# Second buffers for early keys and queries, wider idle matmuls, later stores: one change to an attention and two-MLP kernel

## The chip, the cores and the metric

The kernel runs on one core of one Trainium2 chip. The metric is the device time of one execution in microseconds (us). The kernel before has a median of 1110.62 us over three runs, from 1107.44 to 1112.64.

## What is computed

The reference is chunked local attention with eight memory slots, then two feed-forward layers with different gates, all in float32:

```python
for c in range(nc):                      # 24 chunks of 32 queries
    q_c = q[:, :, c_start:c_end]
    k_full = concatenate([mem_k, k[:, :, l_start:r_end]], axis=2)   # 8 + up to 56 keys
    v_full = concatenate([mem_v, v[:, :, l_start:r_end]], axis=2)
    a = softmax(q_c @ k_full.T / 8)
    out[:, :, c_start:c_end] = a @ v_full
x = out.transpose(0, 2, 1, 3).reshape(3072, 512)
h = x @ w_in1;  x = (s * relu(h) ** 2 + b) @ w_out1           # w_in 512 x 2048, w_out 2048 x 512
h = x @ w_in2;  return (h * sigmoid(1.702 * h)) @ w_out2
```

## The kernel before

**Tiles and blocks.** The 3072 tokens are 24 tiles of 128. Four tiles make a block of 512. The hidden size 2048 is 16 slices `j` of 128 columns. Each slice has a weight tile of w_in and one of w_out.

**Precision.** Every float32 matmul of the feed-forward layers is three matmuls on split operands: a value is cast to a high part, and the rest is subtracted out of it (names that end in h and l, such as `xh`, `xl`, `wih`, `wil`, `gh`, `gl`). So each weight tile has to be prepared: it is loaded as 64-bit words into a ring of three `st` buffers (L326), ScalarE takes an absolute value (L332) and a scaled low word (L342), VectorE clamps (L338), shifts (L346), adds (L350) and puts the sign in (L354), then ScalarE casts the high part (L223) and VectorE subtracts the rest (L312). Working copies `u` have a ring of four.

**Attention.** `attend(u)` does one tile (tiles 0 to 3) or two: load keys, queries, values (L403, all on SyncE's queue except the first two query loads, which ScalarE issues), scores `sc` (L418), row maximum `top` (L435), subtraction into the query buffer `qe` (L438), exponential (L443), transposes `pp` (L451), copy to `px` (L223), sums `den` (L461 to L465), products with the values `o` (L479), normalisation (L484), transposes `xx` (L493), and the split into `xh` and `xl` (L223, L510). `k`, `v`, `qe` and `px` have one buffer each, which holds a pair of tiles `g` = 0, 1, 2, ...: the loads of a pair wait until the pair before is done with the buffer. PSUM is shared too: `sc`, `pp`, `o` and `xx` of tiles 0 and 2 and of all the pairs from (4, 5) on use one region; tiles 1 and 3 use that of the accumulator `accA`.

**First layer.** `step(i)` is a unit: hidden product `ph` of one slice and one block (12 matmuls, L602 to L604), gates `r` (L609, L616, L613 or L620), split `gh`, `gl` (L624, L628), and two units later the output product into `accA` and `accB` (12 matmuls, L640). `VISITS` orders the units: block 0 with slices 0 to 4 (slices 0 and 1 as half blocks, so that tiles 0 and 1 are enough to begin), block 1 with 0 to 4, block 1 with 5 to 15, block 0 with 5 to 15, then blocks 2 and 3. Unit 16 is block 1, slice 9. Blocks 4 and 5 and the whole second layer go through `seven(s)`, a Strassen-like scheme of seven products on prepared w_in slices, which `combine(p)` and `pair(p)` store to DRAM (`wch`, `wcl`) and `stream` reads again.

**Order.** The instruction order of each engine is fixed when the program is built. A planner (class `Plan`) gives each step a due time and a modelled duration and orders all steps; the steps are then emitted in that order on one queue per engine, and each waits only for the data and buffers that it really touches. Where the planner expects TensorE to be idle before the first output product (`plan.first`), it puts in idle matmuls on zeros (L1183), one of 128 columns for each 0.24 us (`BEAT`). `after=` is for the planner: it moves a step in the order and adds no wait of its own.

**What the change touches in `combine`.** For each pair of slices it stores the prepared tiles `wih`, `wil` (L725, four stores: 256, 256, 128 and 128 KB) as soon as they exist, and much later sums them (L736 to L755, two `u` and two `st` buffers) and stores the sums (L764).

**Gates in `seven`.** Two of the four gate sets of each pair of slices (`mine` false) take a `u` buffer for `r` (L999, L1002, L1008), cast and subtract it into a `gq` buffer, and store that to DRAM, except the last sets of a round, which stay in SBUF.

## Time and profile before

| what | value |
|---|---|
| median of three runs | 1110.62 us |
| profiled execution, time | 1112.08 us |
| profiled execution, span in the trace | 1110.2 us |
| TensorE matmul busy | 1088.7 us (98%) |
| VectorE busy | 711.0 us (64%) |
| ScalarE busy | 494.2 us (45%) |
| granted TensorE clock, mean | 1.000 |
| chain that ended last: TensorE's share | 92% |

TensorE is busy in nearly all of the span, so what is left to look at is where it is not, or where it is busy with matmuls on zeros. Both lie almost wholly in the first 82 us, which the rows below show by stretch. A busy TensorE in the profile counts overlapping matmuls, so the view that lists waits is read beside it.

### The profile page before, as it was taken

Reading aid. Unit: us, or ns where it says so; the run is one execution under the profiler, and the core shown is the slowest. Engines: PE = TensorE matmul, PEld = TensorE weight load, DVE = VectorE, ACT = ScalarE, POOL = GpSimd, SP = SyncE. Lnnn points to the kernel's source line nnn. Section 1 sums busy time; section 2 is a strip of 40 time slices with the busy share of each in tenths; the row PEclk is TensorE's granted clock in tenths of the full one; section 3 lists DMA queues with packets and bytes.
Section 4 is the critical chain, followed back from the end, with each engine's and each line's share of the span. In section 5 each row is a group of like instructions: output and inputs, shape, how many; then the busy total and the mean of one; then the engine's idle time right before and its main releaser. Section 6 shows DMA issues by size and latency. Waiting matters only on the chain.

```text
span 1110.2 us, 20092 instructions
## 1 busy us (share of the span) xinstructions
PE 1088.7 (98%) x7852; PEld 897.8 (81%) x7852; DVE 711.0 (64%) x1241; ACT 494.2 (45%) x842; POOL 0.7 (0%) x6
## 2 busy tenths in 40 slices
PE   8879999999999999999999999999999999999998
PEld 7768887888878788888888888888888888888886
DVE  6888988878778688687881455660555760655610
ACT  4678865555445455566640433330433430333310
POOL 0000000000000000000000000000000000000000
PEclk9999999999999999999999999999999999999999
DMA  8776627756678783888999965574755574654154
GB/s 326 245 258 209 208 105 248 259 193 219 208 275 267 265 301 117 312 294 279 318 323 382 322 203 200 183 260 144 246 188 201 202 246 155 203 190 142 76 191 150
DMA packets 119406, 252.99 MB, mean 228 GB/s; under 512 B 12816, under 2 KB 29200, under 8 KB 119312
## 3 DMA queue, kind: packets, MB, share of 16 engines
q1 hardware_dynamic: 119024, 251.19, 66.1%
q8 instruction: 62, 1.02, 0.4%
q10 hardware_dynamic: 288, 0.52, 0.1%
q14 instruction: 32, 0.26, 0.1%
HBM read 169.87 MB, written 81.79 MB: 227 GB/s over the span
## 4 chain that ended last, share of the span: by engine, by line
PE 92%; DMA 3%; DVE 2%; issue 1%; ACT 1%; SPq 0%; ACTq 0%; DVEq 0%
PE accA L1059 16%; PE accB L1059 16%; PE accA L640 7%; PE accB L640 7%; PE ph L981 5%; PE ph L983 5%; PE ph L982 5%; PE ph L602 5%; PE ph L603 5%; PE ph L604 5%; PE pb L983 4%; PE pb L981 4%; PE pb L982 4%; DMA st<-w_in 2%; PE o L479 1%; PE sc L418 1%
## 5 line engine op out<-in xcount | busy, mean ns | idle before, releaser
L997 ACT ACTIVATE r<-ys 128x512 f32<-128x512 f32 x72 | 45.5, 632 | 107.6 <-DVE ys L1094 81.2
L1083 DVE TENSOR_TENSOR ys<-pb,ys 128x512 f32<-128x512 f32 x32 | 22.0, 686 | 91.6 <-DMA out<-y 58.7
L602 PE MATMUL ph<-xh,wih 128*128 128x512 f32 (+1 forms) x200 | 79.3, 396 | 0.6 <-DVE xh L223 0.6
L603 PE MATMUL ph<-xl,wih 128*128 128x512 f32 (+1 forms) x200 | 76.6, 383 | 0.7 <-DVE xl L510 0.7
L604 PE MATMUL ph<-xh,wil 128*128 128x512 f32 (+1 forms) x200 | 76.4, 382 | 0.0
L223 ACT COPY y<-accA 128x512 f32<-128x512 f32 x20 | 10.9, 590 | 138.5 <-issue 84.4
L609 ACT ACTIVATE r<-ph 128x512 f32<-128x512 f32 (+1 forms) x66 | 38.5, 584 | 60.4 <-PE ph L604 54.2
L624 ACT CAST gh<-r 128x512 fp32r<-128x512 f32 (+1 forms) x66 | 40.2, 609 | 47.8 <-PE accB L640 31.2
L1094 DVE TENSOR_TENSOR ys<-pb,ys 128x512 f32<-128x512 f32 x32 | 22.1, 691 | 53.9 <-PE pb L983 53.3
L1006 DVE TENSOR_TENSOR r<-ph,r 128x512 f32<-128x512 f32 x24 | 16.6, 691 | 62.2 <-ACT r L997 62.2
L1059 PE MATMUL accA<-woh,gh 128*128 128x512 f32 x138 | 54.0, 391 | 0.0
L1059 PE MATMUL accA<-woh,gl 128*128 128x512 f32 x138 | 53.9, 390 | 0.0
L1059 PE MATMUL accB<-woh,gh 128*128 128x512 f32 x138 | 53.7, 389 | 0.0
L1059 PE MATMUL accA<-wol,gh 128*128 128x512 f32 x138 | 53.7, 389 | 0.0
L1059 PE MATMUL accB<-woh,gl 128*128 128x512 f32 x138 | 53.7, 389 | 0.0
L1059 PE MATMUL accB<-wol,gh 128*128 128x512 f32 x138 | 53.7, 389 | 0.0
L640 PE MATMUL accA<-gl,woh 128*128 128x512 f32 (+1 forms) x132 | 50.9, 385 | 2.2 <-DVE gl L628 2.2
L1019 ACT CAST gh<-r 128x512 fp32r<-128x512 f32 x64 | 39.8, 622 | 29.1 <-DVE r L1006 21.7
L342 ACT ACTIVATE st<-st 128x512 f32<-128x512 uint32 x64 | 42.8, 676 | 22.4 <-DMA st<-w_out 10.7
L640 PE MATMUL accA<-gh,woh 128*128 128x512 f32 (+1 forms) x132 | 51.4, 389 | 1.3 <-ACT gh L624 1.3
L640 PE MATMUL accB<-gl,woh 128*128 128x512 f32 (+1 forms) x132 | 50.6, 383 | 1.2 <-issue 1.2
L640 PE MATMUL accB<-gh,woh 128*128 128x512 f32 (+1 forms) x132 | 51.0, 387 | 0.0
(210 smaller groups left out, 2973.6 us busy)
## 6 DMA issues: line engine op xcount, KB each, us to landing
gd<-gq SPq DMA_DIRECT2D x56, 512.0 KB, 2.7
wih<-wch SPq DMA_DIRECT2D x96, 256.0 KB, 3.5
wil<-wcl SPq DMA_DIRECT2D x96, 256.0 KB, 3.8
st<-w_in SPq DMA_DIRECT2D x32, 512.0 KB, 5.4
st<-w_out SPq DMA_DIRECT2D x32, 512.0 KB, 5.0
back<-gd SPq DMA_DIRECT2D x56, 256.0 KB, 3.1
k<-k_w SPq DMA_DIRECT2D x24, 512.0 KB, 5.6
v<-v_w SPq DMA_DIRECT2D x24, 512.0 KB, 6.1
```

Of the source, the lines that this page charges most:

```text
L342: nc.scalar.activation(out=lo.bitcast(F32), in_=lo, func=AF.Copy, scale=2.0**-51, bias=2.0)
L602: nc.tensor.matmul(ph, wh, xh, start=(k == 0), stop=False)
L603: nc.tensor.matmul(ph, wh, xl, start=False, stop=False)
L604: nc.tensor.matmul(ph, wl, xh, start=False, stop=(k == KT - 1))
L624: nc.scalar.copy(out=T["g", i][0], in_=T["r", i])
L640: nc.tensor.matmul(o, lt, rh, start=fresh and x == 0, stop=(done and x == 2))
L981: nc.tensor.matmul(ph, wh, xh, start=first and i == 0, stop=False, skip_group_check=True)
L982: nc.tensor.matmul(ph, wh, xl, start=False, stop=False, skip_group_check=True)
L983: nc.tensor.matmul(ph, wl, xh, start=False, stop=i == 1, skip_group_check=True)
L997: nc.scalar.activation(out=T[rk], in_=src(), func=AF.Sigmoid, scale=GATE)
L1019: nc.scalar.copy(out=T[key][0], in_=T[rk])
L1059: nc.tensor.matmul(a, lt, rh, start=n == 0 and x == 0, stop=n == NF - 1 and x == 2)
```

## The change

Six edits; none changes what is computed.

1. Pairs `g` = 1 (tiles 2 and 3) and `g` = 3 (tiles 6 and 7), counted from one the tiles 3, 4, 7 and 8, get a second `k` and `qe` buffer in a pool of their own (`att2`). `v` and `px` stay single.
2. The space of that pool is handed on to the weight tiles `wz` (w_in of slices 12 to 15) when attention of those pairs is done; the preparation of these four tiles now comes after that.
3. Idle matmuls have 512 columns, with one narrower matmul for the rest.
4. `plan.first` is the first four output products, and idle matmuls end before whichever comes first.
5. The four stores of prepared slices of pair `p` (L725) come after the output product of unit 16 + `p`. The sum of the second tile goes into the `st` buffer, where it took a `u` buffer.
6. The last two gate sets of the round `s` = 0 work in place in `ys` and take no `u` buffer.

```diff
-                idle = min(starts[i], starts[self.first]) - clock
+                idle = min(starts[i], *(starts[x] for x in self.first)) - clock
...
+    pool_b = tc.tile_pool(name="att2", bufs=1)
+    sets = [att, pool_b.__enter__()]
+    home = {1: 1, 3: 1}
...
-        d = op(need, {"act": 0.62}, ..., after=[d], alloc=[(tag, w)], uses=[("u", i)])
+        d = op(need, {"act": 0.62}, ..., after=[d] + (o_open if tag == "wz" else []), alloc=[(tag, w)], uses=[("u", i)])
...
-            T[name, g] = att.tile([P, 2, HP, P] if name in ("qe", "px") else [P, 2, HP, CT, D], F32, tag=name, name=name)
+            T[name, g] = (sets[home.get(g, 0)] if name in ("k", "qe") else att).tile([P, 2, HP, P] if name in ("qe", "px") else [P, 2, HP, CT, D], F32, tag=name, name=name)
...
-            return {"alloc": [(name, (name, g))]}
+            return {"alloc": [(name + "1" if name in ("k", "qe") and g in home else name, (name, g))]}
...
+        end_ = [o_unit[16 + p]]
-        done = [op(need, {"sp": 0.75}, keep(v, w0, slice(0, 512), slice(0, 2)), after=first[v:v + 1], uses=[w0]) for v in range(2)]
+        done = [op(need, {"sp": 0.75}, keep(v, w0, slice(0, 512), slice(0, 2)), after=first[v:v + 1] + end_, uses=[w0]) for v in range(2)]
...
+                    T["s", p] = stp.tile([P, 4, 256], F32R, tag="st", name="st")
+                    x = T["s", p].bitcast(F32)[:, 2:4].rearrange("p n d -> p (n d)")
...
+            there = not (mine or away or m)
+                T[rk] = src() if there else (gp if mine else stp).tile(
+                    [P, 512], F32, tag="r" if mine else "u", name="r", bufs=1 if mine else 4)
...
+    o_open.append(op(-1, {"none": 0.0}, follow("att2", "wz", bufs=1), after=two_ops))
...
-            for _ in range(e):
-                nc.tensor.matmul(idle[:, 0, :P], T["cold"], T["cold"], start=True, stop=True)
+            for n in [512] * (e // 4) + ([128 * (e % 4)] if e % 4 else []):
+                nc.tensor.matmul(idle[:, 0, :n], T["cold"][:, :P], T["cold"][:, :n], start=True, stop=True)
```

## Rows read from the trace of the kernel before

**Rows 1.** Busy time by stretch: PE, PEld, DVE, ACT, POOL, PEclk, DMA share, GB/s

```profile
6.80:22.00 15.20, 14.36 (x311) 13.31 (x318) 13.91 (x29) 8.47 (x15) 0.00 (x0) 1.00 1.01 377
22.00:44.65 22.65, 19.81 (x442) 18.25 (x427) 17.09 (x34) 12.10 (x25) 0.00 (x0) 1.00 0.84 273
44.65:81.60 36.95, 28.44 (x567) 22.45 (x566) 32.06 (x57) 28.79 (x51) 0.00 (x0) 1.00 0.74 252
109.70:158.70 49.00, 49.00 (x218) 40.60 (x217) 44.66 (x86) 37.52 (x67) 0.00 (x0) 1.00 0.49 156
...
81.60:1105.80 1024.20, 1020.89 (x6471) 838.89 (x6471) 647.74 (x1122) 442.49 (x750) 0.00 (x0) 1.00 0.65 224
```

**Rows 2.** The same view, idle matmuls of L1183 alone: PE, PEld

```profile
0.00:81.60 81.60, 14.42 (x104) 12.74 (x104) 1.00 0.82 282
```

**Rows 3.** Waits of VectorE, 6.8 to 81.6 us: total us, times, longest

```profile
DVE u L338 <- ACT u L332: 3.3, 2, 2.6
DVE top L435 <- PE sc L418: 2.4, 2, 2.2
```

**Rows 4.** Waits of SyncE's queue, 0 to 82 us

```profile
SPq L326 <- DVE u L354: 16.7, 7, 4.9
SPq L403 <- PE sc L418: 7.8, 4, 3.2
...
SPq L403 <- DVE den L461: 4.4, 2, 3.8
```

**Rows 5.** SyncE in order of time: start, us, what, count

```profile
36.89 0.33 SPq L326 DMA_DIRECT2D st<-w_in  x1
```

**Rows 6.** TensorE in order of time: the scores, with idle time before in brackets

```profile
21.82 1.29 PE L418 MATMUL sc<-k,qe 64*32 64x64 f32 x102
25.71 0.44 PE L418 MATMUL sc<-k,qe 64*32 64x64 f32 x26 [2.60 <-issue]
...
39.50 0.86 PE L418 MATMUL sc<-k,qe 64*32 64x64 f32 x64
...
48.29 0.86 PE L418 MATMUL sc<-k,qe 64*32 64x64 f32 x64
```

**Rows 7.** DMA queues, 23.0 to 23.5 us: packets, MB, share

```profile
q8 instruction: 1, 0.02, 11.9%
```

**Rows 8.** ScalarE and VectorE in order of time, 16 to 81 us

```profile
16.04 0.69 DVE L510 TENSOR_TENSOR xl<-xx,xh 128x512 fp32r<-128x512 f32 x1 [0.36 <-ACT xh L223]
...
33.70 1.29 DVE L510 TENSOR_TENSOR xl<-xx,xh 128x512 fp32r<-128x512 f32 x2
...
43.96 0.66 ACT L332 ACTIVATE u<-st 128x512 f32<-128x512 f32 x1 [3.23 <-DMA st<-w_in]
...
80.25 1.28 DVE L510 TENSOR_TENSOR xl<-xx,xh 128x512 fp32r<-128x512 f32 x2
```

**Rows 9.** DMA issues by line: count, KB each, us to landing; 0 to 81.6, then 81.6 to 158.7

```profile
wch<-wih SPq DMA_DIRECT2D x3, 256.0 KB, 6.7
...
st<-w_in SPq DMA_DIRECT2D x9, 512.0 KB, 4.4
```

**Rows 10.** VectorE's weight preparation to 81.6 us, by group; last row L312 by stretch

```profile
L354 DVE SCALAR_TENSOR_TENSOR u<-st,u 128x512 uint32<-128x512 uint32 x12 | 8.0, 677 | 0.0
L338 DVE TENSOR_SCALAR u<-u 128x512 f32<-128x512 f32 x13 | 5.4, 418 | 3.3 <-ACT u L332 3.3
...
0.00:81.60 81.60, 7.44 (x11) 1.00 0.82 282
```

**Rows 11.** The last w_in tile of block 1: prepared, and first used

```profile
151.95 0.68 DVE L312 TENSOR_TENSOR wzl<-u,wzh 128x512 fp32r<-128x512 f32 x1
...
158.67 0.39 PE L602 MATMUL ph<-xh,wzh 128*128 128x512 f32 x1
```

**Rows 12.** Waits of TensorE after 110 us

```profile
PE xx L493 <- DVE px L484: 1.9, 1, 1.9
...
PE ph L981 <- ACT ys L1081: 0.3, 1, 0.3
```

More of the change, by code (lines that the diff above doesn't have):

```diff
@@ L217, in attention_moe_moe @@
     plan = Plan()
-    plan.first = None
+    plan.first = []
     op = plan.op
@@ L272, in warm @@
         for _ in range(WARM):
-            nc.tensor.matmul(w[:, :P], T["cold"], T["cold"], start=True, stop=True)
+            nc.tensor.matmul(w[:, :P], T["cold"][:, :P], T["cold"][:, :P], start=True, stop=True)
     plan.tag("h", 2)
     op(-999, {"pe": 0.43 * WARM}, warm, after=[o_cold], alloc=[("h", "warm")], uses=["cold"])
-    managers = {"att": pool_a}
+    managers = {"att": pool_a, "att2": pool_b}
     def follow(old, new, **kw):
@@ L314, in prep @@
         d = words(i, w, need)
-        d = op(need, {"act": 0.62}, lambda e: (tiles(e), high(e)), after=[d], alloc=[(tag, w)], uses=[("u", i)])
+        d = op(need, {"act": 0.62}, lambda e: (tiles(e), high(e)), after=[d] + (o_open if tag == "wz" else []), alloc=[(tag, w)], uses=[("u", i)])
         f = op(need, {"dve": 0.62}, rest, after=[d], uses=[("u", i)])
@@ L365, in words @@
         return op(need, {"dve": 0.62}, sign, after=[d], uses=[u, st])
[L368 removed]
+    for n in ("k", "v", "qe", "px", "k1", "qe1"):
         plan.tag(n, 1)
@@ L570, in attend @@
         stage_ops.extend(range(one, len(plan.ops)))
+        if g in home:
+            two_ops.extend(range(one, len(plan.ops)))
     plan.tag("g", 2)
-    o_split, o_y, o_part = {}, {}, {}
+    o_split, o_y, o_part, o_unit = {}, {}, {}, {}
     halves = ("accA", "accB")
@@ L728, in combine @@
         first = list(o_w[w0]) + list(o_w[w1])
-        done = [op(need, {"sp": 0.75}, keep(v, w0, slice(0, 512), slice(0, 2)), after=first[v:v + 1], uses=[w0]) for v in range(2)]
-        done += [op(need, {"sp": 0.4}, keep(v, w1, slice(256, 512), slice(2, 3)), after=first[2 + v:3 + v], uses=[w1]) for v in range(2)]
+        end_ = [o_unit[16 + p]]
+        done = [op(need, {"sp": 0.75}, keep(v, w0, slice(0, 512), slice(0, 2)), after=first[v:v + 1] + end_, uses=[w0]) for v in range(2)]
+        done += [op(need, {"sp": 0.4}, keep(v, w1, slice(256, 512), slice(2, 3)), after=first[2 + v:3 + v] + end_, uses=[w1])
+                 for v in range(2)]
         def whole(w, k):
             def fn(e):
-                T[k, p] = stp.tile([P, 512], F32, tag="u", name="u", bufs=4)
+                if k == "wa":
+                    x = T[k, p] = stp.tile([P, 512], F32, tag="u", name="u", bufs=4)
+                else:
+                    T["s", p] = stp.tile([P, 4, 256], F32R, tag="st", name="st")
+                    x = T["s", p].bitcast(F32)[:, 2:4].rearrange("p n d -> p (n d)")
                 h, l = T[w]
-                nc.vector.tensor_tensor(out=T[k, p], in0=h.bitcast(F32), in1=l.bitcast(F32), op=ALU.add)
+                nc.vector.tensor_tensor(out=x, in0=h.bitcast(F32), in1=l.bitcast(F32), op=ALU.add)
             return fn
@@ L758, in combine @@
         a = op(need, {"dve": 0.65}, whole(w0, "wa"), after=first[:2] + end_, alloc=[("u", ("wa", p))], uses=[w0])
-        b = op(need, {"dve": 0.65}, whole(w1, "wb"), after=first[2:] + end_, alloc=[("u", ("wb", p))], uses=[w1])
-        c = op(need, {"dve": 1.5}, sums, after=[a, b], alloc=[("st", ("s", p))], uses=[("wa", p), ("wb", p)])
+        b = op(need, {"dve": 0.65}, whole(w1, "wb"), after=first[2:] + end_, alloc=[("st", ("s", p))], uses=[w1])
+        c = op(need, {"dve": 1.5}, sums, after=[a, b], uses=[("wa", p), ("s", p)])
         h = op(need, {"act": 1.05}, high, after=[c], alloc=[("st", ("sh", p))], uses=[("s", p)])
@@ L1022, in gate4 @@
                 nc.vector.tensor_tensor(out=T[key][1], in0=T[rk], in1=T[key][0].bitcast(F32), op=ALU.subtract)
-            a = op(need, {"act": 0.6}, gate1, after=d, alloc=[("r" if mine else "u", rk)], uses=uses)
+            a = op(need, {"act": 0.6}, gate1, after=d, alloc=[] if there else [("r" if mine else "u", rk)], uses=uses)
+            here_r = uses if there else [rk]
             last = a
@@ L1028, in gates @@
             else:
-                b = op(need, {"act": 0.6}, square, after=[a], uses=[rk])
-                b = op(need, {"dve": 0.42}, gate2, after=[b], uses=[rk])
+                b = op(need, {"act": 0.6}, square, after=[a], uses=here_r)
+                b = op(need, {"dve": 0.42}, gate2, after=[b], uses=here_r)
             here, kw = [("g", key)], {}
@@ L1037, in gates @@
             own = [] if mine else [box]
-            g1 = op(need, {"act": 0.62}, gate3, after=[b], alloc=here, uses=[rk] + own, **kw)
-            g2 = op(need, {"dve": 0.66}, gate4, after=[g1], uses=[rk] + own)
+            g1 = op(need, {"act": 0.62}, gate3, after=[b], alloc=here, uses=here_r + own, **kw)
+            g2 = op(need, {"dve": 0.66}, gate4, after=[g1], uses=here_r + own)
             if not mine and away:
```

20 lines of the change are left out of this document (9 added, 11 removed).

## The prediction

> **What bounds the kernel now.** I read the busy times by stretch first. From 81.6 us to the end of the matmuls at 1105.8, TensorE is busy 1020.89 of 1024.2 us [rows 1]; its longest wait after 110 us is 1.9 us [rows 12]. No edit removes a matmul there, so the time after 81.6 us can only move as a whole. What can shrink is the stretch before it, which ends when `xl` of tiles 6 and 7 is written (80.25 + 1.28 = 81.5 us [rows 8]) and block 1 can begin. There TensorE runs 104 records of idle matmuls, 14.4 us with overlaps [rows 2], and from 44.65 to 81.6 us it is busy only 28.44 of 36.95 us [rows 1].
>
> Next I looked for what TensorE waits for in that stretch. VectorE is busy 13.91 of 15.2, 17.09 of 22.65 and 32.06 of 36.95 us [rows 1]: 63.1 of 74.8 us, so 11.7 us idle. Part of its work isn't due yet: blocks 0 and 1 with slices 0 to 4 need ten weight tiles, but L338 (and L346, of the same count and time) ran 13 times, L354 (and L350) 12 and L312 11 times [rows 10]. The surplus is 6 x 0.418 + 4 x 0.68 + 0.68 = 5.9 us. So VectorE owes 57.2 us before block 1 can begin, and with no gap it would be done at 6.8 + 57.2 = 64.0 us. This **floor** is 17.6 us below 81.6. Nothing in the change shortens VectorE's own work, so 17.6 us is the most it can bring.
>
> Last I looked at what leaves VectorE idle. Two waits carry most of it: 3.3 us for ScalarE's absolute value and 2.4 us for scores [rows 3]. The first goes back to a w_in load issued at 36.89 us [rows 5] for which ScalarE stood until 43.96 [rows 8], 7.1 us from issue; in the quieter stretch behind 81.6 us such a load lands in 4.4 us [rows 9]. The second is the 2.60 us break in the scores of tiles 2 and 3 [rows 6]. SyncE issues in order, and its waits show why transfers come in bunches: 7.8 us for scores to free `k`, 4.4 us for `den` to free `qe`, 16.7 us for a free `st` buffer [rows 4].
>
> **The change part by part.** *Own buffers (edit 1).* Keys and queries of tiles 2 and 3 can be issued at the start, and those of 4 and 5 as soon as tiles 0 and 1 are done, whom they follow in the first set. Most of the 7.8 + 4.4 us of waits in SyncE's queue goes. The waits for `v` and for `st` stay. What comes late next is PSUM: tile 2's scores need the region that tile 0 leaves at 16.04 + 0.69 = 16.7 us [rows 8], so they can run some 5 us before the 21.82 of [rows 6]. They then no longer stand in one burst with tile 3's. For tiles 4 and 5 the region is free at about 34.3 us (the first of the two `xl` of 33.70 [rows 8]), yet their scores run at 39.50 and 48.29 [rows 6]; loaded early, they can run as soon as it is free. For tiles 6 and 7 nothing is gained by itself.
>
> What that saves, in VectorE's time: of the 3.3 us, all, because the queries and values ahead of the 36.89 us load no longer pile up there (bounds 0 and 3.3). Of the 2.4 us, all, because the burst is broken up (bounds 0 and 2.4). Against them stand the early loads for tiles 2 and 3: 2 x 512 + 2 x 256 KB, 1.5 MB, which go in front of the first weights while the DMA engines are full (share 1.01 at 377 GB/s [rows 1]): 4.0 us later for these weights. I cost this at nothing, because VectorE has tile 2's earlier scores to do meanwhile; without that cover it costs up to 4.0 us.
>
> *Late stores (edit 5).* Three pairs of slices are stored before 81.6 us. Each has a store of 256 KB for the high part [rows 9], one for the low part, and two half as large for its second slice: 3 x 768 KB = 2.3 MB, at 377 GB/s [rows 1] 6 us of transfer, and 12 issues on SyncE. All leave the stretch. Part of this is already in the 3.3 us above, so I add only what lets VectorE change its order: with loads landing sooner it does due work where it now does early preparations. Of the 5.9 us surplus I take 1.5 us (bounds 0 and 5.9; nearer to 0, since the 16.7 us for `st` buffers stay). Where the stores go, from about 140 us on, the DMA share is 0.49 [rows 1]; eight pairs of 768 KB are 2.0 us each, one per unit, beside other work. They add no wait: a store reads weight tiles that are long written. Loads of the last weight tiles that stand behind them in SyncE's queue would pay 2 us each if that cover were gone. The sum in `st` in place of `u` has the same instructions: 0.
>
> *Idle matmuls (edits 3, 4).* They fill expected idle time; the same columns in fewer instructions are worth 0 by themselves. Their instruction count is the point that could matter. The break at 23.1 us contains an instruction packet at 23.0 to 23.5 us [rows 6, 7], while the DMA engines are full, so it looks like TensorE waiting for its code; fewer instructions move where that falls. The Trainium skill ("Runtime: NRT & Kernel Launch", section "Instruction fetch mechanics") says the contrary of such a reading: the sequencer fetches the next 16 KiB block by itself while it runs the current one, so that crossing a block is mostly hidden. By the page the break would have another cause, edit 3 could not touch it, and the sum would lack its 2.4 us unless the split burst alone removes it. I hold to the row.
>
> *`wz` handed on (edit 2).* The first of these four tiles is used three units before the last, far behind block 1's begin; the last is ready at 151.95 + 0.68 = 152.6 us and used at 158.67 [rows 11]. Tiles 6 and 7 are done some 60 us before that, so no wait: 0. *Gates in place (edit 6).* Two gate sets out of a whole round, in a stretch where TensorE's only wait is 0.3 us [rows 12]: 0, bounds 0 and 0.3.
>
> *What comes back.* The slack of the last w_in tile is 158.67 - 152.6 = 6.0 us [rows 11], with VectorE 91% busy there (44.66 of 49.0 [rows 1]). If block 1 begins 7.2 us earlier and 1.5 us of preparation move behind it, 8.7 us are wanted of 6.0 us plus the 4.3 us that VectorE is idle in that stretch. I take 0.7 us lost (bounds 0 and 2.7). The wait of 1.9 us [rows 12] may come out otherwise in a new order: 0, bounds -1.9 and 1.9.
>
> **The sum.** 3.3 + 2.4 + 1.5 - 0.7 = 6.5 us. Against the profiled execution (1112.08 us, of which 1110.2 is the span) that is 1105.6; it ran 1.5 us above the median of 1110.62, so for a median I say **1104.1 us**. Block 1 should begin at about 74.5 us.
>
> **Rivals.** *VectorE and the `st` ring hold it.* The loads come early, but the 16.7 us for `st` [rows 4] still set when weights are ready, and the code stop remains or moves. Then only the late w_in landing is saved, 0 to 3.3 us: about 1109. For it speaks that VectorE is 87% busy from 44.65 us on; against it that the two named waits are on its own list.
> *Near the floor.* With scores of tiles 4 and 5 some 10 us earlier, VectorE always has something due, and most of the surplus and idle goes: 12 of 17.6 us, 1098.6. For it speaks the 14 us from 34.3 to 48.3 us on the chain of the shared PSUM region; against it the 6.0 us slack behind.
> *Slower: early keys in front of the first weights.* The 1.5 MB delay the first weights by 4.0 us in the full stretch. This decides if VectorE then has nothing to do between 10 and 16 us: it can't win that back while the `st` ring paces it. With none of the savings, block 1 begins 4.0 us later: 1114.6, and 1117 with another code stop of 2.6 us.
> *The change doesn't do what it says:* the early issue is certain only in the order of the queue; if SyncE's order still puts weights with waits ahead of these loads, they go out as late as now. That gives the first rival's time.
>
> **How the numbers follow.** Forecast 0.58 (its own range 1101 to 1107.5), first rival with the last 0.22, floor 0.13, slower 0.07. The range must leave out no more than 2 in 10: 1097 to 1111.5 takes in the floor case at 1098.6 and the first rival's no gain with 0.9 us, and leaves out the slower one and the tails. A measurement of this kernel can tell about 0.5%, 5.55 us, from no change: 1105.07 is the border. The forecast's centre lies 1 us below it, so of its 0.58 I give 0.40 to faster and 0.18 to same; the first rival is the same, 0.22; the floor is faster, 0.13; the slower case is split with 0.05 beyond the border and 0.02 within. Faster 0.53, same 0.42, slower 0.05.
>
> **What would show it.** Right: `k` and `qe` of tiles 2 and 3 issued before 8 us; their scores in two pieces, the first by 18 us, without a stop of over 1 us; scores of 4 and 5 in one run before 40 us; no L725 before 130 us; the 3.3 us gone from VectorE's waits; block 1's `xl` near 74 us; TensorE without waits over 3 us in total up to 165 us. Wrong: VectorE's idle time moved to 10 to 17 us; a stop of 2 us or more in a burst of scores; waits of `ph` L602 for L312 between 130 and 160 us; new waits past 280 us.

## The result, and the profile after

The changed kernel takes 1122.5 us (median of four runs, 1119.25 to 1123.59), against 1110.76 us for the kernel before: a ratio of 1.0111, interval 1.0092 to 1.0130. The forecast was 1104.1 us with a range from 1097 to 1111.5; the result is slower than the kernel before by about 12 us, on the other side. The profiled execution took 1119.25 us, its span is 1117.4 us, 7.2 us more than before. It is the fastest of the four, so the trace shows 7 of the 12 us between the medians.

The busy times by stretch answer to [rows 1]; the columns are the same, and the third stretch is cut where block 1 begins, now at 76.6 us:

```profile
6.80:22.00 15.20, 11.77 (x277) 7.93 (x282) 10.34 (x21) 6.56 (x11) 0.00 (x0) 0.89 1.03 398
22.00:44.65 22.65, 21.74 (x451) 17.36 (x447) 19.66 (x39) 14.23 (x29) 0.00 (x0) 1.00 0.73 255
44.65:76.60 31.95, 26.89 (x504) 22.36 (x504) 27.99 (x49) 23.36 (x41) 0.00 (x0) 1.00 0.57 193
76.60:1113.00 1036.40, 1025.62 (x6479) 841.63 (x6478) 652.14 (x1142) 443.13 (x750) 0.00 (x0) 1.00 0.65 224
```

So block 1 begins earlier, by some 4 us (its first hidden product stood at 80.39 us before, the line below, and stands at 76.64 now), and the time is lost behind it: 1036.4 us with 1025.62 us busy, where [rows 1] had 1024.2 with 1020.89. In the first stretch VectorE is busy 10.34 us instead of 13.91, and the granted clock is no longer 1.00.

```profile
80.39 0.50 PE L602 MATMUL ph<-xh,wih 128*128 128x512 f32 x1 [0.64 <-DVE xh L223]
```

To see where the two part, I took TensorE's matmuls without the idle ones in their order and compared the start of the same share of the work in both traces (the alignment). Where the order differs, in the first 110 us above all, this is good to a microsecond or two. The changed kernel is about 1 us late at 42 us, 3.3 us early at 89 us, 4.5 us early at 195 us, 0.9 us early at 359 us (after one wait of 2.9 us at 345 us), 0.2 us late at 560 us, and 7.3 us late at 581 us; that is what it ends with. TensorE's waits after 110 us answer to [rows 12], where the longest was 1.9 us:

```profile
PE accA L1074 <- ACT y L226: 3.8, 1, 3.8
PE sc L421 <- ACT px L226: 2.9, 1, 2.9
```

So there are two questions: why only 3 to 4 us were won at the start, and what happens between 560 and 581 us, where the wait of 3.8 us lies.

The start, in TensorE's order of time, answers to [rows 6]:

```profile
10.98 0.81 PE L482 MATMUL o<-v,px 64*32 64x64 f32 x59
14.38 0.31 PE L482 MATMUL o<-v,px 64*32 64x64 f32 x5 [2.58 <-issue]
14.61 2.01 PE L1199 MATMUL idle<-cold 128*128 128x512 f32 x4
16.41 1.06 PE L454 MATMUL pp<-ident,qe 128*128 128x128 f32 x4
...
20.39 0.67 PE L421 MATMUL sc<-k,qe 64*32 64x64 f32 x42
21.88 0.42 PE L421 MATMUL sc<-k,qe 64*32 64x64 f32 x22 [0.82 <-issue]
...
76.64 0.40 PE L607 MATMUL ph<-xh,wih 128*128 128x512 f32 x1
```

A stop of 2.58 us now stands in the middle of tile 0's products with the values, and tile 2's scores run at 20.39 us, hardly before the 21.82 of [rows 6], with a stop in them too. Behind the first stop four transposes `pp` take 1.06 us; four of them took 0.66 us ahead of it. Two rows say why, the queue of instruction packets in 12.0 to 13.2 us (packets, MB, share), and the stretch from 16 to 18 us, in which the number behind POOL's (x0) is the granted clock:

```profile
q8 instruction: 1, 0.02, 5.8%
```

```profile
16.00:18.00 2.00, 2.00 (x10) 1.80 (x9) 0.95 (x4) 0.00 (x0) 0.00 (x0) 0.50 1.06 394
```

TensorE went on only after a packet of 16 KB of its own code had come, and then ran at half its clock (1.2 instead of 2.4 GHz).

The end of the first round, first TensorE, then ScalarE in order of time:

```profile
572.77 1.22 PE L1074 MATMUL accA<-gq,woh 128*128 128x512 f32 x2 [3.77 <-ACT y L226]
...
579.68 0.73 PE L1074 MATMUL accB<-gq,woh 128*128 128x512 f32 x2 [0.44 <-ACT y L226]
```

```profile
567.68 0.59 ACT L226 COPY y<-accA 128x512 f32<-128x512 f32 x1 [1.00 <-PE accA L1074]
571.61 0.62 ACT L226 CAST st<-u 128x512 fp32r<-128x512 f32 x1 [3.34 <-DVE u L357]
572.13 0.58 ACT L226 COPY y<-accA 128x512 f32<-128x512 f32 x1
574.15 0.62 ACT L226 CAST st<-st 128x512 fp32r<-128x512 f32 x1 [1.43 <-DVE st L803]
578.73 0.41 ACT L226 CAST st<-u 128x256 fp32r<-128x256 f32 x1 [3.97 <-DMA wcl<-st]
579.05 0.58 ACT L226 COPY y<-accB 128x512 f32<-128x512 f32 x1
```

In the kernel before, the copies of the accumulators at the same place are these (VectorE has the one more, at 567.46):

```profile
568.24 0.59 ACT L223 COPY y<-accA 128x512 f32<-128x512 f32 x1 [1.44 <-DVE y L223]
568.84 0.59 ACT L223 COPY y<-accB 128x512 f32<-128x512 f32 x1
```

In the changed kernel a cast of the preparation of `pair(7)` of the second layer (`st<-u`) stands on ScalarE between the two copies of `accA`, and waits 3.34 us for VectorE, which prepares the same pair. The second copy comes at 572.13, and TensorE, which wants to write into `accA` again, waits 3.77 us. Behind that wait the clock is down, 0.70 and 0.62:

```profile
570.00:575.00 5.00, 2.23 (x5) 1.83 (x6) 4.93 (x11) 1.72 (x3) 0.00 (x0) 0.70 0.89 239
575.00:580.00 5.00, 4.56 (x12) 3.28 (x11) 2.23 (x5) 0.89 (x2) 0.00 (x0) 0.62 1.03 390
```

The two rows withhold 5 x 0.30 + 5 x 0.38 = 3.4 us of clock; the trace has the clock at 0.50 from 571.95 to 578.78 us, and the first 0.8 us of that fall into the wait, so 3.0 us of it slow work down. 3.77 us of wait, these 3.0 us and the wait of 0.44 us for `accB` make 7.2 us, the 7.1 us by which the alignment falls back here.

### The profile page after: what moved, and what is told of

Same layout as the page of the kernel before. It is cut to its first block, busy times and chain, and to the rows that moved or that the text cites. A ratio compares the mean times of both kernels' runs of the same rounds, so it can differ in the third digit from the quotient of the medians.

```text
span 1117.4 us, 19888 instructions
## 1 busy us (share of the span) xinstructions
PE 1091.4 (98%) x7780; PEld 894.4 (80%) x7780; DVE 710.6 (64%) x1250; ACT 489.6 (44%) x833; POOL 0.7 (0%) x6
## 4 chain that ended last, share of the span: by engine, by line
PE 85%; DVE 5%; DMA 5%; issue 2%; ACT 1%; SPq 0%; ACTq 0%; DVEq 0%
PE accB L1074 15%; PE accA L1074 15%; PE accA L645 6%; PE accB L645 6%; PE ph L992 5%; PE ph L994 5%; PE ph L993 5%; PE ph L607 4%; PE pb L992 4%; PE ph L609 4%; PE ph L608 4%; PE pb L994 4%; PE pb L993 4%; DMA wcl<-st 2%; DMA st<-w_out 1%
## 5 line engine op out<-in xcount | busy, mean ns | idle before, releaser
L226 ACT COPY y<-accA 128x512 f32<-128x512 f32 x22 | 11.9, 590 | 136.3 <-PE accA L1074 76.3
L645 PE MATMUL accA<-gh,wol 128*128 128x512 f32 (+1 forms) x132 | 50.7, 384 | 0.2 <-DVE wol L315 0.2
L992 PE MATMUL pb<-xl,wih 128*128 128x512 f32 x128 | 50.1, 392 | 0.5 <-DVE ys L1116 0.5
```

The source lines that it names most:

```text
L645: nc.tensor.matmul(o, lt, rh, start=fresh and x == 0, stop=(done and x == 2))
L992: nc.tensor.matmul(ph, wh, xh, start=first and i == 0, stop=False, skip_group_check=True)
```

## The experiments

All stand beside runs of the kernel before. In those that keep single edits, edit 4 and the `after` of edit 2 stay in: the trace of e8, which has both, shows the same order on TensorE, VectorE and ScalarE as the kernel before, idle matmuls aside.

| run | what it is | median us (range) | ratio to before (interval) |
|---|---|---|---|
| e1 | the change without late stores | 1122.17 (1119.69 to 1125.61) | 1.0109 (1.0080 to 1.0138) |
| e2 | late stores alone | 1118.47 (1116.68 to 1120.43) | 1.0078 (1.0052 to 1.0104) |
| e3 | the change, idle matmuls of 128 columns | 1119.80 (1114.56 to 1124.16) | 1.0086 (1.0057 to 1.0116) |
| e4 | the change, pair 7 held | 1114.74 (1112.78 to 1118.24) | 1.0041 (1.0024 to 1.0059) |
| e5 | late stores alone, pair 7 held | 1109.07 (1103.14 to 1113.65) | 0.9992 (0.9971 to 1.0013) |
| e6 | e4 with idle matmuls of 128 columns | 1111.91 (1110.10 to 1115.50) | 1.0025 (1.0009 to 1.0040) |
| e7 | early keys (edits 1, 2) alone | 1107.53 (1104.16 to 1109.05) | 0.9980 (0.9965 to 0.9995) |
| e8 | wide idle matmuls alone | 1117.03 (1114.09 to 1119.33) | 1.0073 (1.0046 to 1.0099) |
| e13 | e8, code moved | 1109.40 (1107.32 to 1112.72) | 0.9998 (0.9984 to 1.0011) |
| e14 | the kernel before, code moved | 1114.22 (1110.02 to 1117.33) | 1.0037 (1.0017 to 1.0056) |
| e15 | e4, code moved | 1106.65 (1104.72 to 1110.44) | 0.9972 (0.9959 to 0.9985) |
| e16 | e5 with wide idle matmuls, code moved | 1106.57 (1105.14 to 1108.99) | 0.9974 (0.9962 to 0.9987) |
| e17 | the whole change, code moved, nothing held | 1111.91 (1110.25 to 1115.61) | 1.0032 (1.0019 to 1.0045) |
| e18 | early keys and wide idle matmuls, code moved | 1110.42 (1108.41 to 1113.78) | 1.0022 (1.0011 to 1.0034) |

### Single edits undone or done alone

**e1, the late stores undone.**

```diff
-        end_ = [o_unit[16 + p]]
+        end_ = []
```

> The changed kernel with one part undone: the four stores of prepared slices go out as soon as the slices exist, as before; all else stays changed, the sum in the st buffer too. In the built order the preparation of the last slice pair (pair 7 of layer 2) then no longer stands among the four copies of y out of accA and accB at the end of the first Strassen round. Theory A (late stores shift that preparation to the round's end, where ScalarE and VectorE take it before the copies and TensorE stands for 3.8 us and then runs at half clock): no wait over 1 us between 540 and 600 us, granted clock 1.00 there, and the 7.1 us lost at that place are gone: time about 1122.5 - 7 = 1115 or less. Rival B (early keys and queries are the cause, the stores are not): the wait of 3.8 us stays, 1121 to 1124. The first 80 us tell how much of the early gain hangs on the stores: if block 1 begins at 76 to 77 us as in the changed kernel, nothing; if at 80 us or later, most of it.

The median didn't move, where I had expected 1115 us or less. The copies at the end of the round are nearly in time again: one wait of 1.6 us there in place of 3.77, and no fall of the clock. Three of TensorE's waits in this run:

```profile
PE pp L454 <- ACT qe L446: 6.4, 1, 6.4
PE sc L421 <- issue: 5.6, 3, 2.9
PE o L482 <- issue: 4.8, 2, 3.2
```

Of the 10.4 us of `issue`, 9.2 stand in the first 43 us. Block 1 begins at 80.6 us as in the kernel before, 4 us later than in the changed one, and at 160 us by the alignment the run is only 1.1 us late against the kernel before; at 250 us it is 11.6 us late. Between lies the wait of 6.4 us, with the clock at half from 195 to 209 us behind it (first TensorE, then VectorE, then the stretch):

```profile
200.06 1.97 PE L454 MATMUL pp<-ident,qe 128*128 128x128 f32 x8 [6.44 <-ACT qe L446]
```

```profile
192.60 0.69 DVE L748 TENSOR_TENSOR st<-wih,wil 128x512 f32<-128x512 f32 x1 [2.94 <-DMA wcl<-st]
...
196.38 1.23 DVE L438 TENSOR_REDUCE top<-sc 128x16 f32<-128x1024 f32 x1
```

```profile
200.00:205.00 5.00, 3.78 (x136) 3.38 (x136) 3.80 (x8) 2.51 (x5) 0.00 (x0) 0.50 0.40 123
```

It looks like the same kind of loss as at the round's end, though no run undoes it. VectorE stands 2.94 us for a store out of an `st` buffer before it takes a sum of prepared slices, the sum that edit 5 puts into `st`. The row maximum of scores that were done at 193.6 us has its place in the order behind that sum and five steps more. So most of the loss at the round's end hangs on the late stores, and without them another place is as dear.

**e2, the late stores alone.**

```diff
-    ... after=first[v:v + 1], uses=[w0]) for v in range(2)]
+    ... after=first[v:v + 1] + [o_unit[16 + p]], uses=[w0]) for v in range(2)]
```

> The kernel before with one part of the change alone: late stores of the prepared slices. In the built order the preparation of pair 7 then stands among the last gates and copies of the first Strassen round on ScalarE. Theory A: TensorE waits 3 us or more between 540 and 600 us, clock below 1.00 behind it, 5 to 9 us lost there: with 0 to 3 us won in the first 80 us, 1113 to 1120. Rival B (stores harmless): no such wait, 1107 to 1112.

By the alignment this kernel is 7 to 9 us early at 114 us and 9.5 us early at 440 us, and block 1's first hidden product stands at 72.31 us: the late stores alone bring more than I gave the whole change. Then it loses 2.9 us between 440 and 560 us and 11.8 us at the end of the round. Its wait there, and the stretch after it:

```profile
PE accA L1071 <- ACT gq L1030: 9.0, 1, 9.0
```

```profile
570.00:580.00 10.00, 8.86 (x25) 6.80 (x26) 2.59 (x6) 2.36 (x4) 0.00 (x0) 0.63 0.94 305
```

**e3, narrow idle matmuls in the changed kernel.**

```diff
-            for n in [512] * (e // 4) + ([128 * (e % 4)] if e % 4 else []):
-                nc.tensor.matmul(idle[:, 0, :n], T["cold"][:, :P], T["cold"][:, :n], ...)
+            for _ in range(e):
+                nc.tensor.matmul(idle[:, 0, :P], T["cold"][:, :P], T["cold"][:, :P], ...)
```

> The changed kernel with idle matmuls of 128 columns again; the order of every engine is otherwise the same, row for row. Theory C (wider idle matmuls bring a code block's end sooner, so TensorE stands 2.6 us at 11.8 us for code and its clock falls to half from 15.2 to 19 us): the stop in the products of tile 0 shrinks to about 0.7 us, granted clock 1.00 throughout the first 30 us, block 1 begins 2 to 4 us sooner, time 1118 to 1120.5 against 1122.5 of the changed kernel. Rival D (the stop comes from the early key loads that fill the DMA engines, whatever the idle matmuls): a stop of 2 us or more in the same burst and a clock below 1.00, time within 1.5 us of the changed kernel. The loss at 570 us stays in both.

2.7 us better than the change by the median, which lies within the spread of its runs (1114.56 to 1124.16). The stop that I had expected to shrink is still there; only the clock stayed up behind it (1.00 from 10 to 20 us):

```profile
15.17 0.42 PE L482 MATMUL o<-v,px 64*32 64x64 f32 x21 [2.75 <-issue]
```

### The end of the round: pair 7 held

**e4** orders the preparation of pair 7 behind the four copies:

```diff
+    for i in o_held:                    # the steps of pair(7), second layer
+        plan.ops[i][3].extend(o_free[:KT])   # after the copies of accA, accB at the round's end
```

> The changed kernel with nothing undone; only the preparation of pair 7 is held, in the planned order, until the four copies of y at the end of the first Strassen round are placed. Theory A: the copies run at once, no wait over 1 us between 540 and 600 us, clock 1.00 there; 7 us less than the changed kernel, about 1115.5. If the loss had another cause than this order (stores' traffic, buffers), the wait stays or moves and the time is 1120 or more.

The wait is gone; ScalarE makes both pairs of copies in a row:

```profile
565.74 1.08 ACT L226 COPY y<-accA 128x512 f32<-128x512 f32 x2 [0.99 <-PE accA L1080]
567.10 1.07 ACT L226 COPY y<-accB 128x512 f32<-128x512 f32 x2 [0.28 <-PE accB L1080]
```

1122.5 to 1114.7: the order at the end of the round is worth 7.8 us of the changed kernel's loss.

**e5** does the same to the late stores alone (the edit of e2 and that of e4).

> The kernel before with the late stores alone (edit 5's `after`), and with the preparation of pair 7 of the second layer ordered behind the four copies of the accumulators at the end of the first round. Theory A (late stores bring about 8 us before 115 us, and lose them again only because the order then puts pair 7 ahead of these copies): no wait of over 2 us of the output products of L1071 at 560 to 580 us, granted clock 1.00 there, and 1102 us (1100 to 1105), 6 to 10 us under the kernel before. Rival (TensorE's gain is given back somewhere else whatever stands there, since ScalarE and VectorE are what really limits the second part): the wait reappears between 560 and 760 us, and 1107 to 1112 us.

The median is 7 us above what I had expected. The round's end is clean, but the start isn't. e5 and e2 have the same order of instructions up to 541 us, and yet the same stop took 0.82 us in e2 (first line) and 3.10 us in e5 (second):

```profile
13.36 0.42 PE L482 MATMUL o<-v,px 64*32 64x64 f32 x21 [0.82 <-issue]
```

```profile
14.52 0.42 PE L482 MATMUL o<-v,px 64*32 64x64 f32 x21 [3.10 <-issue]
```

Its 11 runs reach from 1103.1 us with a mean granted clock of 1.000 to 1113.7 us with 0.995. So the length of a stop seems to differ from run to run, and the profiled one is only an example; only one run of each kernel has a trace.

**e6** is e4 with the narrow idle matmuls of e3.

> The whole change with pair 7 held as in e4, and idle matmuls of 128 columns in place of 512. If the wide idle matmuls cost some 2.4 us by the clock that falls after a stop, it is 2 to 3 us under e4_hold_pair7: 1112.3 us (1110 to 1113.5), and the start is 6 us ahead of the kernel before at the first hidden product of block 1. If the width is worth nothing, it is e4's 1114.7 (1113.5 to 1117). Beside e5_late_stores_held it prices the early keys when the late stores are there: 2 us by the alignment of e2 and e3, so 2 to 3 us over e5; if the early keys cost 8 us and more, as e1 shows them without late stores, it stands at e5 + 8.

Again 2.8 us from the width alone, in a kernel that is otherwise e4, and here clear of the spread of the runs.

### The early keys and the wide idle matmuls alone

**e7**, edits 1 and 2 on the kernel before:

```diff
+    home = {1: 1, 3: 1}
```

> The kernel before with the own buffers for keys and queries of tiles 3, 4, 7 and 8 alone (and the space handed on to `wz`). Theory B (the early keys put 1.5 MB in front of the first weights, so VectorE stands idle between 10 and 20 us, and nothing is won back while the stores of prepared slices still run): block 1 begins 2 to 6 us later than before, VectorE busy under 11.5 us of 15.2 from 6.8 to 22 us, and 1114 to 1122 us. Rival, which is the first term of the forecast (the wait for the late w_in load and the stop in the scores both go): block 1 begins 3 to 6 us earlier and 1104 to 1108 us.

My second theory, that the early keys are what hurts, fell: VectorE is busy 12.93 of 15.2 us from 6.8 to 22 us, block 1's first hidden product stands at 71.43 us instead of 80.39, and the median is 2.2 us better. Of 7 to 9 us in hand at 154 us, 3.3 us are left at the end; they go in several small waits, the largest these:

```profile
PE pp L454 <- ACT qe L446: 2.6, 2, 1.4
PE xx L496 <- DVE px L487: 1.6, 1, 1.6
```

**e8**, edit 3 on the kernel before (the diff of e3 the other way round).

> The kernel before with idle matmuls of 512 columns alone; the order of all other instructions stays. Theory C (fewer instructions stand between two blocks of TensorE's code, so the stops of over 1 us come with less cover, and the granted clock falls after one): a stop of 2.5 us or more before 25 us, the granted clock at 0.50 for 1 to 3 us behind it, and 1112 to 1114 us. Rival (the width alone is worth nothing, and the fall of the clock in the changed kernel comes from its other order): clock 1.00 through the first 82 us and 1110.3 us (1109 to 1111.5).

Seven microseconds slower from an edit that I had costed at nothing. The profiled execution is the fastest of the five (1114.09 us), so its trace shows the kind of loss and not the whole of it. By the alignment, which is exact here since the order is that of the kernel before, it is 0.6 us early at 30 us and 4.6 us late at 35 us, and ends 2.1 us late. In it a stop of 2.52 us ends at 15 us, with the clock at 1.00 behind it, and a stop of 3.85 us stands in the products of tiles 2 and 3 with the values; an instruction packet lies in 32.2 to 33.3 us, and the clock is 0.71 behind it:

```profile
29.44 1.51 PE L482 MATMUL o<-v,px 64*32 64x64 f32 x123
34.80 0.43 PE L482 MATMUL o<-v,px 64*32 64x64 f32 x5 [3.85 <-issue]
```

```profile
35.00:40.00 5.00, 5.00 (x20) 2.81 (x15) 2.90 (x6) 1.65 (x3) 0.00 (x0) 0.71 0.76 219
```

### Where the code is cut

I numbered the matmul records of TensorE in order of time. In all these traces the stops of `issue` stand ahead of the same numbers: 221, 348, 476, 602 or 603, 730, 857, 1111, 1367, that is 126 to 128 apart, or twice that (single records can be missing in a trace). The kernel before stops at 221, 476 and 1367 (1.22 us, at 77.5 us), the changed one at 221, 348, 602 and 1111, e8 at 221, 603 and 1112. So TensorE's code comes in pieces of 128 records, one packet of 16 KB each: over the whole changed kernel the queue has 61 packets (the line below) for 7780 records, 127.5 each. At four of the stops I took the times: TensorE goes on 5.0 to 7.4 us after it had passed the end of the piece before (before: 7.54 to 12.56 us; changed: 8.86 to 14.38; e8: 28.70 to 34.80; e5: 7.08 to 14.52). From this comes a theory: a piece that is worked off in less than about 6 us, as one full of 64-column matmuls of 12 ns is, ends in a stop. Wide idle matmuls are fewer records (6 where the kernel before has 18 at 7 us), so all later ends fall elsewhere. Taking the stops out of e8's times and shifting the ends, I got 11.5 us of stops for e8 as it is and about 1 us with 88 records more in front; for the kernel before 4.3 us as it is, 11.9 us with 68 more. In the traces, the four have 7.2, 2.1 (e13), 4.5 and 5.2 us (e14) of such stops.

```profile
q8 instruction: 61, 1.00, 0.4%
```

The theory is right about the place and not about the rule. In all traces there are 41 stops of `issue` of over 0.5 us, and 39 of them end 1.1 to 1.6 us after the end of such a packet, at the end of a piece. But I counted twelve pieces in each of the 16 traces other than those of e9 to e12: 72 were worked off in under 6 us, and 34 of these ended in a stop of over 0.5 us, 38 did not; of the 120 slower ones, two did. And from one end to the next, a piece with a stop took 2.2 to 7.9 us over these traces, not 5.0 to 7.4. A fast piece is nearly a condition for a stop. What decides if one comes and how long it is is when the packet lands, and no run here isolates what sets that.

**e9 to e12** were to test this by small matmuls on zeros at the very start in place of ten wide ones:

```diff
-        for _ in range(WARM):
-            nc.tensor.matmul(w[:, :P], T["cold"][:, :P], T["cold"][:, :P], ...)
+        for _ in range(WARM + 88):       # 68 in e10
+            nc.tensor.matmul(w[:32, :64], T["cold"][:64, :32], T["cold"][:64, :64], ...)
```

> The kernel of e8 (wide idle matmuls alone), with the ten matmuls on zeros at the very start (128 columns each, 1.1 us) replaced by 98 small ones of the form of the scores (12 ns each, 1.2 us): the same time, but every later instruction stands 88 matmuls further on in TensorE's code. Theory C2 (a stop of `issue` comes where TensorE reaches the end of a stretch of 128 matmuls of its code less than about 6 us after it reached the end of the stretch before; the width only moves these ends into the dense bursts of 64-column matmuls): no such stop of over 1 us in the first 82 us, granted clock 1.00 there, 1107 us (1105 to 1110), about 10 us under e8's 1117. Rival (the wide matmuls are slow by themselves, by the clock or by what they do to the stretch): 1114 to 1119 us again.

> The kernel before, with nothing changed but the ten matmuls on zeros at the very start: 78 small ones of the form of the scores in the same 1 us, so that every later instruction stands 68 matmuls further on in TensorE's code. By theory C2 the ends of the stretches of 128 matmuls then fall at about 10 us (stop of 2 us or more), 30 us (3 us or more) and 47 to 53 us (3 us or more), with the clock falling behind some of them: 1115 us (1112.5 to 1120), as e8. Rival (where the code is cut plays no part): 1110 us (1108.5 to 1111.5).

> The whole change with pair 7 held (the kernel of e4, 1114.7 us), and the code moved on by 88 matmuls as in e9. If the round's end (about 8 us) and the places of the code's cuts (theory C2: 4 to 7 us of stops and half clock) are together the whole loss of the changed kernel: 1108.5 us (1106 to 1111). Rival (the early keys and the other edits cost by themselves, so that only 2.8 us are to be had, as e6's narrow idle matmuls brought): 1112 us or more.

> The kernel of e5 (late stores, pair 7 held; 1109.1 us with runs from 1103.1 to 1113.7) with wide idle matmuls and the code moved on by 88 matmuls. By theory C2 the stop of 3.1 us at 14 us in e5 is gone, the clock stays at 1.00, and the start is 8 us ahead of the kernel before at 114 us, as it was in e2, where that stop was 0.8 us: 1102 us (1100 to 1105), with a spread of runs under 6 us. This would beat both kernels. Rival (e5's spread comes from elsewhere, such as the end of the round): 1107 to 1110 us with the same spread.

They failed as experiments. All write to one place of the array, so they don't overlap: 0.108 us per record, not 0.012, and each counts as two records. In e9:

```profile
2.18 21.01 PE L276 MATMUL warm<-cold 64*32 64x64 f32 x195
```

The first scores stood at 18 to 23 us instead of 6. The four took 1124.62, 1121.44, 1123.25 and 1125.78 us, and say nothing on the question.

**e13 to e16** go round four places of the array, so that the small matmuls fit into the time of the ten (3.20 us, where the ten take 3.67 us before and 4.47 in e8):

```diff
+        for n in range(WARM + 44):       # 34 in e14
+            r, c = slice(32 * (n % 4), 32 * (n % 4) + 32), 64 * (n // 4 % 8)
+            nc.tensor.matmul(w[r, c:c + 64], T["cold"][:64, :32], T["cold"][:64, :64], ...)
```

> The kernel of e8 (wide idle matmuls alone, 1117.0 us), with the ten matmuls on zeros at the very start (20 records, 3.7 to 4.5 us) replaced by 54 small ones (108 records) that go round four places of the array, so that they should fit into the same time, and every later instruction stands 88 records further on in TensorE's code. Theory C2 (a stop of `issue` comes where TensorE reaches the end of a stretch of 128 records of its code less than about 6 us after the end of the stretch before): no such stop of over 1 us from 12 to 82 us, granted clock 1.00 there, 1107.5 us (1105 to 1110.5). Rival (the wide matmuls cost by themselves): 1114 to 1119 us. If the small matmuls end after 6.4 us, where the first scores stood, the time that they end later is to be taken off.

The products that stopped for 3.85 us in e8 run through, and there is no stop of over 0.5 us before 68 us:

```profile
27.06 1.56 PE L483 MATMUL o<-v,px 64*32 64x64 f32 x128
```

At the same width 7.6 us are gone, from 1117.0 to 1109.4. (A stop of 2.05 us, ending at 70.8 us, is left, ahead of record 1367, with the clock at 0.66 from 70 to 75 us; my 82 us were too far.)

> The kernel before, with nothing changed but the ten matmuls on zeros at the very start: 44 small ones in their place, so that every later instruction stands 68 records further on. By theory C2 the ends of the stretches of 128 records then fall so that stops of 2 us and more stand at about 9 us (scores of tile 1), 30 us and 47 us or 56 us, with the clock falling behind some of them: 1115 us (1112.5 to 1120). Rival (the place where the code is cut plays no part): 1110 us (1108 to 1111.5).

The other way round: the kernel before, with no edit of the change, gets 4.8 us slower than its own 1109.42 us in the runs beside it. One stop is at the second place that I had worked out, ahead of record 731; the other two are missing, and one of 0.82 us stands at 61 us. An instruction packet lies in 32.5 to 33.7 us:

```profile
29.95 0.60 PE L1184 MATMUL idle<-cold 128*128 128x128 f32 x3
34.88 1.44 PE L1184 MATMUL idle<-cold 128*128 128x128 f32 x5 [4.33 <-issue]
```

```profile
35.00:40.00 5.00, 5.00 (x27) 5.00 (x28) 2.02 (x4) 1.95 (x4) 0.00 (x0) 0.59 0.30 113
```

Could the new beginning itself be what costs? The scores of tile 1 do come 1.9 us later than before (10.94 against 9.09 us), because the idle matmuls behind the small ones took 4.21 us and not 2.28. But the products of tiles 2 and 3 with the values come 1.6 us earlier (first the kernel before, then e14):

```profile
30.02 1.51 PE L479 MATMUL o<-v,px 64*32 64x64 f32 x128 [0.24 <-ACT px L223]
```

```profile
28.46 1.56 PE L480 MATMUL o<-v,px 64*32 64x64 f32 x128
```

The order of both is the same, so the alignment is exact: 1.4 us early at 28 us, 3.7 us late at 35 us, 5.1 us late at 40 us, 4.5 us late at the end. The loss comes with this one stop and the half clock behind it. The sum of the stops alone (5.2 us, against 4.5 before) would not tell it: their place counts, and what the clock does behind them.

> The whole change with pair 7 held (the kernel of e4, 1114.7 us), with the code moved on by 88 records as in e13. If the end of the round (7.8 us) and the places of the code's ends are together nearly the whole loss of the changed kernel: 1109 us (1106.5 to 1111.5). Rival (the places are worth no more than the 2.8 us that narrow idle matmuls brought in e6): 1112 us or more.

> The kernel of e5 (late stores, pair 7 held; 1109.1 us, runs from 1103.1 to 1113.7) with wide idle matmuls and the code moved on by 88 records. By theory C2 the stop of 3.1 us at 14 us is gone, the clock stays at 1.00, and block 1 begins some 8 us ahead of the kernel before, as in e2 where that stop was 0.8 us: 1102.5 us (1100 to 1105.5), faster than both kernels. Rival (the early part is ruled by VectorE, and e5's median is what late stores are worth): 1107 to 1110 us.

Both are faster than the kernel before, by 0.28% (0.15 to 0.41) and 0.26% (0.13 to 0.38), and so than the changed one. e16 keeps less of its gain than I expected, 4 us less, but its runs lie within 3.9 us where e5's lay within 10.5. In e15 block 1's first hidden product stands at 73.13 us.

**e17 and e18** ask if the two causes add up, and what the early keys are worth with the ends out of the way.

> The whole change as it is (1122.5 us), nothing held, with the code moved on by 88 records as in e13 and e15. If the end of the round and the places of the code's ends are two causes that add up, moving the code alone takes off the 8.1 us between e4 and e15: 1114.4 us (1112 to 1117), with the wait of the output products at about 565 us still there. Rival (they are one cause, since what the early stops delay is what comes late at the end of the round): 1110 us or less, with that wait gone; or the places matter only when the round's end does not: 1119 us or more.

> The kernel before with the early keys (e7, 1107.5 us), wide idle matmuls, and the code moved on by 88 records. Against the early keys' own rival (that their 2 us in e7 are only a better place of the code's ends): with the code placed well they should be under e13 (1109.4 us) by 2 to 4 us, 1106 us (1104 to 1107.5), and with e16 (1106.6) and e15 (1106.7) among the fastest. If the early keys are worth nothing by themselves, 1109 us as e13.

e17: moving the code alone takes 10.6 us off the whole change. The wait at the end of the round is as it was, with the clock at 0.83 over the ten microseconds:

```profile
564.74 1.22 PE L1075 MATMUL accA<-gq,woh 128*128 128x512 f32 x2 [3.77 <-ACT y L226]
```

So they are two causes: 1122.5 to 1111.9 by the code and on to 1106.65 by holding pair 7, or 1114.7 by holding first and 8.1 us by the code. They don't add up quite: 10.6 and 7.8 us each alone, 15.9 together. e17's clock at 0.83 withholds 1.7 us, where the changed kernel's two rows withheld 3.4, and with pair 7 held (e4, e5, e15, e16) TensorE waits 1.7 us for ScalarE at about 613 us, where e17 waits 0.3. e18 comes out 1.0 us above e13, 4 us over what I expected, with stops of 1.5 to 1.6 us again at 24, 35 and 41 us and one of 2.0 us at 344: here the ends do not fall well, so the run doesn't price the early keys by themselves.

## Why the prediction was wrong

Two steps failed: edit 3 at "0 by themselves", with only a gain put on what its instruction count moves, and edit 5 with "They add no wait". In their place the runs show 10.6 us for where the ends of the code fall (e17) and 7.8 us for pair 7 in front of the four copies (e4). With both undone (e15) the change is 2.8 us faster than the kernel before, where the sum has 6.5 us.

**The place of the gain.** That VectorE's owed work sets the begin of block 1 held: it was busy 58.0 us from 6.8 us to that point in the changed kernel (10.34 + 19.66 + 27.99) and 58.05 us in e15, where I had worked out 57.2. Its parts were mis-sized. The surplus that I let shrink by 1.5 us went almost whole, 5 us; the idle time that I let shrink by 5.7 us stayed: 11.8 us of 69.8, as against 11.7 before. The late absolute value costs 1.5 us instead of 3.3 [rows 3], half of what was foreseen, and VectorE now waits for the scores that TensorE brings late:

```profile
DVE sc L428 <- PE sc L421: 7.3, 2, 5.5
DVE u L341 <- ACT u L335: 1.5, 1, 1.5
```

With the code moved (e15) block 1 begins 7.3 us earlier than before, and the first hidden product stands at 73.13 us where I had said 74.5 for its begin. So the begin of block 1 would have come as forecast, but for the stops. That the total fits is partly luck: VectorE's surplus gave 5 us instead of 1.5, and its idle time in e15 shrank to 66.3 - 58.05 = 8.2 us, by 3.5 us instead of 5.7. The late stores, for which only the 1.5 us stood, bring block 1 forward by 8.1 us alone (e2, 72.31 against 80.39).

**Edit 3 costed at nothing: the first step that failed.** I had read the stop of [rows 6, 7] as a wait for code and named the instruction count as what could matter, and then put 2.4 us of gain and no loss on it. Alone it cost 7.3 us (e8); in the changed kernel going back to narrow ones gained 2.7 us (e3, within its spread) and 2.8 us (e6), and leaving them wide with the code moved gained 10.6 us (e17). What was missing is a bound below nothing: the stop can move to a dearer place as well as go away. The Trainium skill ("Runtime: NRT & Kernel Launch", section "Instruction fetch mechanics") gives blocks of 16 KiB, which the packets here agree with, and says that crossing one is mostly hidden; here the trace disagrees, with stops of up to 4.33 us, and moving the ends alone is worth 4.8 to 10.6 us (e14, e17).

**Edit 5: "they add no wait".** True of the stores: they are issued from 137.3 us on, and none waits for data.

```profile
L731 SPq DMA_DIRECT2D wch<-wih x12: 319/455/1039, 137.3 to 165.3; - x12
```

But `after=` moves steps in the planner, and the planner then placed all later preparations anew; pair 7 came to stand in front of the four copies that free the accumulators. I had looked for what the stores meet in SyncE's queue, and not for what their new place does to the order on ScalarE and VectorE 400 us later. It cost 7.8 us (e4), and 11.8 us by the alignment in e2. e1 has what looks like a second such place, with 6.4 us of wait from 194 us on and a sum that waits for `st` in front, the part of this edit that I had at 0. That "the time after 81.6 us can only move as a whole" was the sentence that closed this off.

**Edit 1.** Keys and queries of tiles 2 and 3 were issued from 5.5 to 8.6 us, about as said, but tile 2's scores stood at 20.39 us, not before 18. Alone the edit brought block 1 9.0 us forward (e7), more than I gave it; at the end of the run 2.2 us were left. With the code moved it was 1.0 us slower than without the early keys (e18 beside e13), with four stops of 1.5 us and more, where e13 has one. So the largest worth that a run shows is 2.2 us, its worth without stops stays open, and I had 5.7 us for it. What comes back I had at 0.7 us (0 to 2.7): e15 gave back about 2, e7 about 5.

**Edits 2, 4, 6** at nothing: no run prices 6 by itself, nor the sum in `st`. 2 without the buffers, and 4, leave the orders of the three engines alone (e8).

**The rivals.** The slower one (early keys in front of the first weights) had its sign in the trace: VectorE idle between 10 and 20 us, busy 10.34 of 15.2 us. But with the same early keys and the code moved it was busy 12.86 us (e17), and e7 alone was faster. The sign came from TensorE's stops, not from the weights, and 1114.6 to 1117 was not far enough. The code stop stood in it only as 2.6 us on top, and no rival had the order at the end of the round.

## What to carry to other kernels

Where a kernel has bursts of very short matmuls while transfers run, an edit that changes how many instructions stand in front of them may not be free: count the records, mark every 128th, and see which burst the ends fall into, or move them on purpose with matmuls on zeros and measure. Where a planner writes the order, an `after` put on one step moves others: look in the new order at each place where an accumulator or a buffer is freed, however far behind, for steps that stand in front of the copy and wait for something else. And price an edit both alone and undone, since here the early keys, the late stores and the width were each worth several microseconds more or less in other company.

## What the runs showed of the hardware

- The same order of instructions stops for 0.82 us or 3.10 us at the same record (e2, e5), and for 1.42 us or not at all (ahead of record 348 in e3 and e6). The place sets where a stop can stand, not if one comes nor how long it is. TensorE went on 1.2 to 1.6 us after the packet's end (13.16 to 14.38 us in the changed kernel, 33.22 to 34.80 in e8, 33.56 to 34.88 in e14).
- A full DMA load is no condition: around e8's stop of 3.85 us the data queue's share was 68.2% (32.2 to 33.3 us), around that of the changed kernel 97.9%.
- A fall of the granted clock to 0.50 followed the 2.58 us stop of the changed kernel, but none came after 2.75 us in e3 or 2.60 us before [rows 6]; in e13 one came with a stop of 2.05 us. What decides it was not settled.
- A matmul of 64 x 64 on zeros took 0.108 us per record on one place of the array, 0.030 us when four places take turns (3.20 us for 108), and 0.012 us in the scores.
